# Taking two units' own terms from feature rows: a fused attention and two-layer product kernel on one core

## The chip, the core and the metric

The kernel runs on one core of a Trainium2 chip. The core has five engines with a queue each: PE (matrix products), DVE (vector), ACT (scalar functions and copies), POOL (a second vector engine) and SP, which here only issues transfers. Sixteen DMA engines carry the transfers. The metric is the device time of one execution in microseconds. Three runs of the kernel before gave 769.85, 770.53 and 771.16 us; the median is 770.53.

## What is computed

The reference has three parts. First a linear attention with a decaying state, for 4 batches of 8 heads, 768 steps, 48 features:

```python
state = zeros((B, H, D, D))
for t in range(S):
    kt, vt, rt, wt = k[:, :, t], v[:, :, t], r[:, :, t], w[:, :, t]
    cur = einsum('bhd,bhe->bhde', u[None] * kt, vt)
    y[:, :, t] = einsum('bhd,bhde->bhe', rt, state + cur)
    state = wt[..., None] * state + einsum('bhd,bhe->bhde', kt, vt)
```

Then, on the 3072 rows of the result with 384 columns, `((x @ w1) * (x @ w2) @ w3) @ w_out` with 1024 inner columns, and on what that gives, `max(x @ v1, x @ v2, x @ v3) @ v_out` with 768 inner columns. The weights come in 64 bits.

The step's *own term* is what `cur` adds to `y[t]`: the sum over the features of r·k·u at step t, times v at step t. The change is about how this one number for each step and head is found.

## The kernel before

**Units.** The attention is cut into eight units of 384 steps (half a batch each), and a unit into four pairs of heads (`j` = 0 to 3; k0 to k3 below means the four pairs of a unit, written `k = (u, j)` in the code). Within a pair, 384 steps are six chunks of 64. The two heads of a pair stand in partitions 0 to 47 and 64 to 111.

**Feature rows.** `dm` is one tile per pair with a row for each feature: the decays w, the keys k (in reversed order of time) and the queries r (forward). It is loaded by two DMAs of 48 rows (L303), each row 1159 numbers long. DVE scans the decays backwards (`sf`, L345) and forwards (`e`, L352); POOL multiplies keys (`kk`, L356) and queries (`x1`, `x2`, L370 and L372) by them.

**Token rows.** `tok` is a second copy of r and k, with a row for each step (128 partitions, 2304 bytes each), loaded at L312. POOL forms r·k (`rk`, L314) and r·k·u (`rku`, L316); a sum over each row gives six numbers per partition, `c`: on DVE in one instruction (L329), or, in unit 1 alone (`DIAG_ACT`), on ACT in six (L327). POOL then writes them on the diagonal of each chunk's 64 x 64 matrix, which stands in the free half of `x1` and `x2` (`dg0`, `dg1`, L380).

**Products of a pair.** PE forms the chunk matrices (`qk`, L392 and L393), DVE copies their lower triangles beside the diagonal (L405), PE transposes `kk` (`tr`, L398) and forms the states (`u`, L459), and at last the outputs (`y`, L417 and L418), which go in two parts to `xT` (L427, L428). The fourth pair's outputs go to `xT` by DMA (`xp`, L435).

**Weights.** At the start, `w3` and `w_out` are multiplied with each other once (`wmul`, L826): 64 products of 128x384 in full f32, two for each of the eight pieces of `w3`, called halves below (four products each). They need the three `wo` tiles (two for the first half, the third for the second) and a piece of `w3`. Each of these 1024-column tiles is made from 64-bit words by three DVE instructions (L784, L787, L790). `w1` and `w2` (`w12`) follow in eight tiles, each in two parts of 384 columns, with a copy on ACT (L817) and a subtraction on POOL (L818).

**The long products.** For each unit and each of eight column tiles PE forms two groups of nine products (`Aa`, `Ab`, from `xT` and `w12`) and one of nine (`B`, from `gs` and `W`); a first product of unit u needs all of `xT`. After the last unit the second layer's groups (C and D) follow. All of these come from one helper and stand at L509.

**What sets the order.** All instructions are recorded as events with an engine, an estimated cost, what they need, what buffers they claim and, for some, a due time. A planner (`Plan`, L48) walks through them in a time of its own and writes each engine's instructions in the order of their start there. On the chip each engine then works through its own list in that order, and waits at the head of the list. Its constants are numbers in the code: the rate it assumes for a transfer (`RATE`), and the due times (`T_A`, `UNIT`, `T_W`, `D_W`, `LEAD`, `T_V`). A change of any of them can move instructions on all engines. SP's transfers are in that same order.

Of the kernel before, what the change touches and what calls it, by code (L numbers as in the profile page):

```python
# [9 lines left out]
F32 = mybir.dt.float32  # L10
# [21 lines left out]
O_K, O_R = NW, NW + T  # L32
DMW = NW + 2 * T

# [13 lines left out]
class Plan:  # L48
# [5 lines left out]
    HOP = 0.12  # L54
    RATE = 285e3
    LAND = 3.0
# [154 lines left out]
class Net:  # L211
# [4 lines left out]
    def constants(self, pool):  # L216
# [46 lines left out]
    NX = 4  # L263
    DIAG_ACT = (1,)

# [8 lines left out]
    def plan_unit(self, u):  # L274
# [10 lines left out]
        for j in range(NJ):  # L285
# [3 lines left out]
            def dm(k=k):  # L289
                return self.dm[slot["dm", *k][0]]  # L290
# [14 lines left out]
            add(("dm", *k), "SP", 1.0, load, after=last, size=96 * DMW * 4,  # L305
                claims=[("dm", [(w, *k) for w in ("sf", "e", "x1", "x2", "kk", "wchk0", "wchk1")])])
            lt = [("tok", u, j - 1)] if j else [("tok", u - 1, NJ - 1)] if u else []
# [8 lines left out]
            add(("rku", *k), "POOL", 0.80, lambda k=k: G.tensor_mul(  # L316
                tok(k)[:, 0], tok(k)[:, 0], self.ub[:, k[1], :].unsqueeze(1).to_broadcast([128, NC, D])),
                [("rk", *k)], lock=True)

            def cd(k=k):  # L320
                return self.cd[slot["diag", *k][0]]

            def diag(k=k):
                if k[0] in self.DIAG_ACT:
                    for c in range(NC):
                        t = tok(k)[:, 0, c]
                        SC.activation(out=t, in_=t, func=AF.Copy, accum_out=cd(k)[:, c:c + 1])  # L327
                else:
                    V.tensor_reduce(out=cd(k), in_=tok(k)[:, 0], axis=AX.X, op=ALU.add)  # L329

            add(("diag", *k), *(("ACT", 1.6) if u in self.DIAG_ACT else ("DVE", 0.45)), diag,
                [("rku", *k)], claims=[("c", [("dg0", *k), ("dg1", *k)])])

# [32 lines left out]
            def r(k, p, q):  # L366
                return dm(k)[p:q, O_R:].rearrange("p (c t) -> p c t", t=C)

# [659 lines left out]
def layout(inputs):  # L1028
# [10 lines left out]
    for i, h in enumerate((1, 0)):  # L1039
# [4 lines left out]
        rd[:, :, i] = rows(R)  # L1044
    dm = np.concatenate([x.reshape(NU, NJ, 2 * D, -1) for x in (we, kd, rd)], axis=3)
    tok = np.stack([R[:, :, :, :, ::-1], K[:, :, :, :, ::-1]], axis=2)
# [17 lines left out]
    res["u2"] = u2  # L1064
    res |= {"dm": dm, "tok": tok, "v1": v1, "v2": v2, "u": ub, "w3": w3, "wo": wo, "w12": w12}
    for n in ("moe_w1", "moe_w2", "moe2_w1", "moe2_w2", "moe2_w3", "moe2_w_out"):
# [20 lines left out]
```

## Time and profile before

| | |
|---|---|
| median of three runs | 770.53 us |
| the profiled execution | 770.51 us |
| its span, first to last instruction | 768.7 us |
| mean granted share of PE's clock | 0.983 |
| PE busy | 737.4 us, 96% of the span |
| weight loads on PE | 696.9 us, 91% |
| DVE, ACT, POOL busy | 447.0, 332.9, 243.5 us |
| moved by DMA | 102.94 MB, mean 134 GB/s |

The span is cut in 40 slices in this part of the page; a digit is the busy share in tenths, and PEclk is the clock granted to PE in tenths of full speed:

```
PE   3499999999999999999999999999999999999996
DVE  7798999677876777585547887323232323232222
PEclk8689999999999999999999999999999999999999
DMA  7988753445354543344024447576767200000001
```

A slice is 19.2 us. PE is filled from the third slice to the last but one, and DVE is above 70% in the first six; the DMA engines are busiest in the first four. The two levels of PE's clock are 1.2 GHz (0.5 in the profile) and 2.4 GHz (1.0).

### The profile page before, as it was taken

Reading aid. Unit: us, or ns where it says so; the run is one execution under the profiler, and the core shown is the slowest. Engines: PE = TensorE matmul, PEld = TensorE weight load, DVE = VectorE, ACT = ScalarE, POOL = GpSimd, SP = SyncE. Lnnn points to the kernel's source line nnn. Section 1 sums busy time; section 2 is a strip of 40 time slices with the busy share of each in tenths; the row PEclk is TensorE's granted clock in tenths of the full one; section 3 lists DMA queues with packets and bytes.
Section 4 is the critical chain, followed back from the end, with each engine's and each line's share of the span. In section 5 each row is a group of like instructions: output and inputs, shape, how many; then the busy total and the mean of one; then the engine's idle time right before and its main releaser. Section 6 shows DMA issues by size and latency. Waiting matters only on the chain.

```text
span 768.7 us, 14960 instructions
## 1 busy us (share of the span) xinstructions
PE 737.4 (96%) x5994; PEld 696.9 (91%) x5994; DVE 447.0 (58%) x731; ACT 332.9 (43%) x798; POOL 243.5 (32%) x293
## 2 busy tenths in 40 slices
PE   3499999999999999999999999999999999999996
PEld 1366788999999999999999999999999999999996
DVE  7798999677876777585547887323232323232222
ACT  2244556354635445354343335667766422222211
POOL 4484678655575565545002332000000000000000
PEclk8689999999999999999999999999999999999999
DMA  7988753445354543344024447576767200000001
GB/s 252 308 274 251 218 185 85 109 110 151 98 139 126 126 93 111 92 125 93 2 82 172 129 159 280 197 256 204 245 204 242 76 32 1 32 1 32 1 31 35
DMA packets 30588, 102.94 MB, mean 134 GB/s; under 512 B 4272, under 2 KB 7472, under 8 KB 30512
## 3 DMA queue, kind: packets, MB, share of 16 engines
q1 hardware_dynamic: 30368, 101.72, 43.2%
q8 instruction: 49, 0.80, 0.4%
q14 instruction: 27, 0.22, 0.1%
q10 hardware_dynamic: 144, 0.20, 0.1%
HBM read 91.28 MB, written 8.26 MB: 129 GB/s over the span
## 4 chain that ended last, share of the span: by engine, by line
PE 93%; DVE 5%; issue 1%; POOL 1%; DMA 0%; ACT 0%; SPq 0%; DVEq 0%; POOLq 0%
PE bank L509 40%; PE rot L509 38%; PE bank L826 6%; PE bank L417 3%; PE bank L392 2%; PE bank L459 1%; PE bank L398 1%; PE bank L393 1%; DVE conv L784 1%; DVE x L405 1%; DMA dm<-in_dm 0%; DVE conv L787 0%; DVE e L352 0%; POOL w L818 0%; DVE gs L856 0%
## 5 line engine op out<-in xcount | busy, mean ns | idle before, releaser
L509 PE MATMUL rot<-xT,w 128*128 128x384 f32 x1152 | 217.2, 339 | 0.9 <-POOL w L818 0.7
L509 PEld LDWEIGHTS rot<-xT,w 128*128 128x128 f32 x1152 | 198.6, 188 | 4.3 <-POOL w L818 1.3
L509 PE MATMUL bank<-x2s,v 128*128 128x384 f32 x684 | 125.6, 336 | 0.0
L509 PEld LDWEIGHTS bank<-x2s,v 128*128 128x128 f32 x684 | 119.0, 188 | 0.0
L509 PE MATMUL bank<-gs,W 128*128 128x384 f32 x576 | 112.6, 338 | 1.2 <-DVE gs L856 1.2
L509 PEld LDWEIGHTS bank<-gs,W 128*128 128x128 f32 x576 | 100.7, 188 | 2.5 <-DVE gs L856 1.8
L956 DVE TENSOR_TENSOR m<-m,bank 128x384 f32<-128x384 f32 x58 | 32.1, 554 | 109.2 <-PE bank L509 99.9
L509 PE MATMUL bank<-vo,ms 128*128 128x384 f32 x432 | 83.5, 337 | 0.0
L509 PE MATMUL rot<-x2s,v 128*128 128x384 f32 x450 | 83.5, 336 | 0.0
L509 PEld LDWEIGHTS rot<-x2s,v 128*128 128x128 f32 x450 | 78.4, 188 | 0.0
L509 PEld LDWEIGHTS bank<-vo,ms 128*128 128x128 f32 x432 | 76.5, 187 | 0.2 <-DVE ms L963 0.2
L961 ACT CAST ms<-m 128x384 fp32r<-128x384 f32 x48 | 24.6, 513 | 96.7 <-DVE m L956 96.4
L850 ACT COPY a<-rot 128x384 f32<-128x384 f32 x64 | 30.6, 478 | 77.6 <-PE rot L509 77.4
L956 DVE TENSOR_TENSOR m<-m,rot 128x384 f32<-128x384 f32 x38 | 21.0, 554 | 66.9 <-PE rot L509 61.0
L854 ACT CAST gs<-g 128x384 fp32r<-128x384 f32 x64 | 32.9, 515 | 61.9 <-DVE g L852 60.3
L852 DVE TENSOR_TENSOR g<-a,rot 128x384 f32<-128x384 f32 x64 | 35.3, 551 | 41.4 <-PE rot L509 40.9
L356 POOL TENSOR_TENSOR kk<-dm,sf 112x384 f32<-112x384 f32 x32 | 32.0, 1006 | 62.3 <-PE bank L393 26.7
L405 DVE COPY_PREDICATED x<-later,bank 64x384 f32<-64x384 uint32 x64 | 37.9, 592 | 22.8 <-PE bank L393 21.8
L826 PE MATMUL bank<-wo,piece 128*128 128x384 f32 x128 | 46.9, 525 | 3.4 <-DVE piece L790 3.4
L856 DVE TENSOR_TENSOR gs<-g,gs 128x384 fp32r<-128x384 f32 x64 | 41.0, 642 | 15.0 <-ACT gs L854 14.8
L370 POOL TENSOR_TENSOR x<-dm,e 48x384 f32<-48x384 f32 x32 | 30.9, 966 | 44.5 <-DVE e L352 27.1
L826 PEld LDWEIGHTS bank<-wo,piece 128*128 128x128 f32 x128 | 25.7, 206 | 21.0 <-DVE piece L790 3.5
(117 smaller groups left out, 1080.1 us busy)
## 6 DMA issues: line engine op xcount, KB each, us to landing
dm<-in_dm SPq DMA_DIRECT2D x64, 217.3 KB, 4.1
tok<-in_tok SPq DMA_DIRECT2D x32, 288.0 KB, 4.0
wst<-in_w SPq DMA_DIRECT2D x8, 1024.0 KB, 8.7
top<-in_w SPq DMA_DIRECT2D x8, 1024.0 KB, 5.0
vst<-in_moe_w SPq DMA_DIRECT2D x9, 768.0 KB, 4.7
top<-in_moe_w SPq DMA_DIRECT2D x9, 768.0 KB, 4.4
wst<-in_w SPq DMA_DIRECT2D x8, 768.0 KB, 5.2
top<-in_w SPq DMA_DIRECT2D x8, 768.0 KB, 4.2
```

The costliest lines, as they stand in the source:

```text
L356: add(("kk", *k), "POOL", 0.86, lambda k=k: G.tensor_mul(kk(k).rearrange("p (c t) -> p c t", t=C), dm(k)[0:PR, O_K:O_R].rearrange("p (c t) ...
L370: add(("x1", *k), "POOL", 0.94, lambda k=k: G.tensor_mul(x1(k)[64:PR], r(k, 64, PR), e(k)[64:PR, :, 0:C]), [("e", *k)], after=lx, lock=Tru ...
L405: add((f"qk{i}", *k), "DVE", 0.59, lambda k=k, x=x, p=p: V.copy_predicated(x(k)[p:p + 64], self.later.bitcast(U32)[p:p + 64].unsqueeze(1). ...
L417: nc.tensor.matmul(ps[0:48, s], self.TA[:, o], x1(k)[:, c, :], start=True, stop=True)
L509: r = self.nc.tensor.matmul(ps, w[p], x[q], start=first and i == 0, stop=last and i == 2)
L826: nc.tensor.matmul(ps[:, 0:DM], t[:, jt * 128:(jt + 1) * 128], wo[:, jt * DM:jt * DM + DM], start=jt == 0, stop=jt == FT - 1)
L850: add(("a", g), "ACT", 0.48, lambda g=g: SC.copy(at[slot["a", g][0]], rot[slot["Aa", g][0]][:, 0:T]), [("Aa", g)], claims=[("a", [("m", g)])])
L852: add(("m", g), "DVE", 0.555, lambda g=g: V.tensor_mul(gt[slot["m", g][0]], at[slot["a", g][0]], rot[slot["Ab", g][0]][:, 0:T]), [("a", g) ...
L854: add(("h", g), "ACT", 0.51, lambda g=g: SC.copy(gst[slot["h", g][0]][:, 0], gt[slot["m", g][0]]), [("m", g)], claims=[("gs", [("B", g)])])
L856: add(("l", g), *self.on("l", u, 0.56, 0.95), lambda g=g, u=u: self.eng("l", u).tensor_sub(gst[slot["h", g][0]][:, 1], gt[slot["m", g][0]] ...
L956: V.tensor_max(t, t, p)
L961: add(("mh", h), "ACT", 0.51, lambda h=h: SC.copy(p2["ms"][slot["mh", h][0]][:, 0], p2["m1"][slot["mx", h, 0][0]]), [("mx", h, 2)], claims ...
```

## The change

For units 0 and 1 (`DIAG_PE`) the token copy is no longer loaded. POOL multiplies the keys of `dm` by its queries, read backwards, to a tile of 112 x 384 (`rk`, in the space of `tok`). PE multiplies each chunk of it with a column of u by features (`dp`: twelve products per pair, 48 rows, 64 columns of weights, one moving column), which lands in PSUM as six numbers per step row; ACT copies them to `c`. The other units keep their way, and all of them now sum on DVE. A small tile `uf` with u by features is loaded first. A row of `dm` is filled up with zeros from 1159 to 1184 numbers. The planner's rate and due times are changed too.

```diff
-DMW = NW + 2 * T
+DMW = (NW + 2 * T + 31) // 32 * 32
-    RATE = 285e3
+    RATE = 380e3
-    DIAG_ACT = (1,)
+    DIAG_PE = (0, 1)
...
-            add(("tok", *k), "SP", 0.55, lambda k=k: nc.sync.dma_start(tok(k), a["tok"][k]), after=lt,
-                size=128 * 2 * NC * D * 4, claims=[("tok", [("diag", *k)])])
-            add(("rk", *k), "POOL", 0.80, lambda k=k: G.tensor_mul(tok(k)[:, 0], tok(k)[:, 0], tok(k)[:, 1]),
-                [("tok", *k)], lock=True)
...
+            if u in self.DIAG_PE:
+                def rk(k=k):
+                    return self.tok[slot["rk", *k][0]].rearrange("p a c d -> p (a c d)")[0:PR, 0:T]
+
+                add(("rk", *k), "POOL", 0.95, lambda k=k: G.tensor_mul(
+                    rk(k), dm(k)[0:PR, O_K:O_R], dm(k)[0:PR, O_R + T - 1:O_R - 1:-1]), [("dm", *k)], after=lt, lock=True,
+                    claims=[("tok", [("dp", *k)])])
+
+                def dp(k=k):
+                    ps = self.ab[slot["dp", *k][0]]
                     for c in range(NC):
...
+                        q = slice(T - c * C - C, T - c * C)
+                        nc.tensor.matmul(ps[0:64, c:c + 1], rk(k)[64:PR, q], self.uf[64:PR, k[1]:k[1] + 1], start=True, stop=True)
+                        nc.tensor.matmul(ps[64:128, c:c + 1], rk(k)[0:48, q], self.uf[0:48, k[1]:k[1] + 1], start=True, stop=True)
+
+                add(("dp", *k), "PE", 0.35, dp, [("rk", *k)], claims=[("ab", [("diag", *k)])], kind="s")
+                add(("diag", *k), "ACT", 0.2, lambda k=k: SC.copy(cd(k), self.ab[slot["dp", *k][0]][:, 0:NC]), [("dp", *k)],
+                    claims=[("c", [("dg0", *k), ("dg1", *k)])])
+            else:
...
-    T_A, UNIT, T_W, D_W, LEAD, T_V = 29.5, 37.7, 18.9, 2.0, (1.0, 16.9, 3.6, 35.2), 20.0
+    T_A, UNIT, T_W, D_W, LEAD, T_V = 32.8, 38.3, 20.5, 3.1, (0, 16.9, 5.1, 35.2), 10.0
...
+        nc.sync.dma_start(self.uf, a["uf"])
         nc.sync.dma_start(self.ub, a["u"])
```

**SP, from the start.** `wst` is a tile of 64-bit weights (from `wo` or `w3`, shown as `in_w`), `dm` the feature rows of a pair, `V`, `TA` and `TB` the values, `tok` the token rows. Before:

```order
L743 DMA ub_96<-in_u 128x192
L303 DMA dm_128<-in_dm 48x1159 x2
L303 DMA dm_129<-in_dm 48x1159 x2
L758 DMA wst_121<-in_wo 128x2x512
L758 DMA wst_122<-in_wo 128x2x512
L758 DMA wst_123<-in_w 128x2x512
L441 DMA V_151<-in_v 128x1152
L312 DMA tok_130<-in_tok 128x576
L312 DMA tok_131<-in_tok 128x576
L445 DMA TA_152<-in_v 64x1152
L446 DMA TB_153<-in_v 64x1152
```

The same place with the change:

```order
L758 DMA uf<-in_uf 112x4
L759 DMA ub_97<-in_u 128x192
L774 DMA wst_122<-in_wo 128x2x512
L304 DMA dm_129<-in_dm 48x1184 x2
L304 DMA dm_130<-in_dm 48x1184 x2
L774 DMA wst_123<-in_wo 128x2x512
L774 DMA wst_124<-in_w 128x2x512
L456 DMA V_152<-in_v 128x1152
L460 DMA TA_153<-in_v 64x1152
L461 DMA TB_154<-in_v 64x1152
L774 DMA wst_122<-in_wo 128x2x512
L774 DMA wst_123<-in_w 128x2x512
```

The first weight tile now stands ahead of the feature rows, the two token loads are gone, and the third `wo` tile and the second piece of `w3` follow at once.

**SP, the rows that follow**, where the feature rows of k2 and k3 of unit 0 are loaded. Before:

```order
L303 DMA dm_128<-in_dm 48x1159 x2
L758 DMA wst_121<-in_wo 128x2x512
L303 DMA dm_129<-in_dm 48x1159 x2
L758 DMA wst_122<-in_w 128x2x512
L758 DMA wst_123<-in_w 128x2x512
```

With the change, behind the rows shown above:

```order
L774 DMA wst_124<-in_w 128x2x512
L304 DMA dm_129<-in_dm 48x1184 x2
L774 DMA wst_122<-in_w 128x2x512
L304 DMA dm_130<-in_dm 48x1184 x2
L774 DMA wst_123<-in_w 128x2x512
```

The rows of k2 (`dm_129`) stand behind two more weight tiles than before, and those of k3 (`dm_130`) behind three more.

**DVE, after the first memsets.** `conv`, `wo` and `piece` are the three steps of a weight tile, `sf`, `inv` and `e` the scans of a pair. Before:

```order
L345 SCALAR_TENSOR_TENSOR sf_134<-dm_128,first 112x390
L350 RECIPROCAL inv_76<-sf_134 112x6
L352 SCALAR_TENSOR_TENSOR e_132<-dm_128,inv_76 112x390
L345 SCALAR_TENSOR_TENSOR sf_135<-dm_129,first 112x390
L350 RECIPROCAL inv_77<-sf_135 112x6
L352 SCALAR_TENSOR_TENSOR e_133<-dm_129,inv_77 112x390
L784 TENSOR_SCALAR conv<-wst_121 128x1024
L787 SCALAR_TENSOR_TENSOR conv<-wst_121,conv 128x1024
L790 SCALAR_TENSOR_TENSOR wo<-wst_121,conv 128x1024
L784 TENSOR_SCALAR conv<-wst_122 128x1024
```

With the change:

```order
L800 TENSOR_SCALAR conv<-wst_122 128x1024
L803 SCALAR_TENSOR_TENSOR conv<-wst_122,conv 128x1024
L806 SCALAR_TENSOR_TENSOR wo<-wst_122,conv 128x1024
L360 SCALAR_TENSOR_TENSOR sf_135<-dm_129,first 112x390
L360 SCALAR_TENSOR_TENSOR sf_136<-dm_130,first 112x390
L800 TENSOR_SCALAR conv<-wst_123 128x1024
L803 SCALAR_TENSOR_TENSOR conv<-wst_123,conv 128x1024
L806 SCALAR_TENSOR_TENSOR wo<-wst_123,conv 128x1024
L365 RECIPROCAL inv_76<-sf_135 112x6
L800 TENSOR_SCALAR conv<-wst_124 128x1024
L803 SCALAR_TENSOR_TENSOR conv<-wst_124,conv 128x1024
L806 SCALAR_TENSOR_TENSOR piece_125<-wst_124,conv 128x1024
```

The first weight tile is made ahead of the first scan, and the two `e` scans now follow the first piece of `w3`.

## Rows read from the trace of the kernel before

**Rows 1.** The page's first part: busy time of each engine, its share, instructions.

```profile
PE 737.4 (96%) x5994; PEld 696.9 (91%) x5994; DVE 447.0 (58%) x731; ACT 332.9 (43%) x798; POOL 243.5 (32%) x293
```

**Rows 2.** Stretches of the span: busy time of each engine, granted clock, DMA.

```profile
core 0: us, PE busy (x) PEld busy (x) DVE busy (x) ACT busy (x) POOL busy (x), PEclk, DMA share, GB/s
0.00:10.00 10.00, 5.51 (x8) 2.31 (x8) 5.15 (x15) 1.56 (x2) 2.90 (x14) 1.00 0.54 116
10.00:20.00 10.00, 1.33 (x6) 0.80 (x7) 9.69 (x10) 3.37 (x12) 5.97 (x6) 0.59 1.01 398
22.00:24.00 2.00, 0.00 (x0) 0.00 (x0) 1.93 (x3) 0.26 (x1) 1.92 (x3) 0.50 1.05 229
24.00:26.00 2.00, 1.09 (x2) 0.79 (x3) 1.58 (x3) 0.00 (x0) 0.69 (x3) 0.50 1.00 180
30.00:40.00 10.00, 3.78 (x51) 2.86 (x48) 9.17 (x11) 2.40 (x7) 4.52 (x5) 0.78 1.03 326
100.00:140.00 40.00, 37.71 (x475) 34.49 (x475) 34.33 (x57) 20.21 (x50) 34.59 (x44) 1.00 0.45 127
350.00:500.00 150.00, 150.00 (x1107) 148.24 (x1106) 95.21 (x138) 65.85 (x132) 31.87 (x24) 1.00 0.42 140
```

**Rows 3.** The chain that ended last, to 90 us: start, duration, work.

```profile
24.91 4.76 PE bank L826 x8
...
38.74 7.09 PE bank L826 x16
...
49.45 0.20 PE bank L392
...
50.99 5.36 PE bank L826 x16
56.35 0.29 PE bank L398 x3
...
65.29 20.84 PE bank L826 x64
```

**Rows 4.** DVE in order of time: start, duration, work, idle time before and its releaser.

```profile
8.43 0.97 DVE L345 TENSOR_TENSOR_SCAN sf<-dm,first 112x390 f32<-112x390 f32 x1 [3.01 <-DMA dm<-in_dm]
...
13.58 1.20 DVE L784 TENSOR_SCALAR conv<-wst 128x1024 uint32<-128x1024 uint32 x1
...
17.33 1.23 DVE L784 TENSOR_SCALAR conv<-wst 128x1024 uint32<-128x1024 uint32 x1
...
41.36 1.22 DVE L790 SCALAR_TENSOR_TENSOR piece<-wst,conv 128x1024 uint32<-128x1024 uint32 x1
```

**Rows 5.** Groups of instructions by line: count, then busy us and mean ns.

```profile
L345 DVE TENSOR_TENSOR_SCAN sf<-dm,first 112x390 f32<-112x390 f32 x32 | 36.8, 1150 | 8.4 <-DMA dm<-in_dm 8.4
L352 DVE TENSOR_TENSOR_SCAN e<-dm,inv 112x390 f32<-112x390 f32 x32 | 36.8, 1149 | 0.7
...
L356 POOL TENSOR_TENSOR kk<-dm,sf 112x384 f32<-112x384 f32 x32 | 32.0, 1006 | 62.3 <-PE bank L393 26.7 <-DVE sf L345 24.2 <-PE rot L509 5.9
...
L329 DVE TENSOR_REDUCE c<-tok 128x6 f32<-128x288 f32 x28 | 12.3, 445 | 3.6 <-POOL x L380 2.5 <-POOL tok L316 1.0
```

**Rows 6.** SP's queue in order of time: start, duration, transfers issued.

```profile
4.11 2.12 SPq L303 DMA_DIRECT2D dm<-in_dm  x4
...
7.25 0.47 SPq L758 DMA_DIRECT2D wst<-in_w  x1
...
15.25 0.98 SPq L303 DMA_DIRECT2D dm<-in_dm  x2
```

**Rows 7.** Transfers issued from 6 to 9 us: count, KB each, us to landing.

```profile
wst<-in_w SPq DMA_DIRECT2D x1, 1024.0 KB, 11.2
```

**Rows 8.** Transfers issued from 13 to 16 us, likewise.

```profile
dm<-in_dm SPq DMA_DIRECT2D x2, 217.3 KB, 10.7
```

**Rows 9.** The chain: the first work behind unit 1's last outputs.

```profile
123.99 1.77 PE rot L509 x9
```

**Rows 10.** SP's queue: the transfers of unit 1's last outputs.

```profile
125.60 3.71 SPq L435 DMA_DIRECT2D xT<-y  x6
```

More of the change, by code (lines that the diff above doesn't have):

```diff
@@ L242, in constants @@
         self.ub = pool.tile([128, NJ, D], F32, name="ub")
+        self.uf = pool.tile([PR, NJ], F32, name="uf")
     def att_tiles(self):
@@ L305, in plan_unit, with first @@
             add(("dm", *k), "SP", 1.0, load, after=last, size=96 * DMW * 4,
-                claims=[("dm", [(w, *k) for w in ("sf", "e", "x1", "x2", "kk", "wchk0", "wchk1")])])
-            lt = [("tok", u, j - 1)] if j else [("tok", u - 1, NJ - 1)] if u else []
+                claims=[("dm", [(w, *k) for w in ("sf", "e", "x1", "x2", "kk", "wchk0", "wchk1") + ("rk",) * (u in self.DIAG_PE)])])
+            def first(u):
+                return "rk" if u in self.DIAG_PE else "tok"
+            lt = [(first(u), u, j - 1)] if j else [(first(u - 1), u - 1, NJ - 1)] if u else []
@@ L320, in cd @@
             def cd(k=k):
                 return self.cd[slot["diag", *k][0]]
-            def diag(k=k):
-                if k[0] in self.DIAG_ACT:
-                    for c in range(NC):
[L326 to L332, printed above, removed]
+            if u in self.DIAG_PE:
[6 more added lines that the diff above has]
+                    ps = self.ab[slot["dp", *k][0]]
+                    for c in range(NC):
+                        q = slice(T - c * C - C, T - c * C)
[5 more added lines that the diff above has]
+            else:
+                add(("tok", *k), "SP", 0.55, lambda k=k: nc.sync.dma_start(tok(k), a["tok"][k]), after=lt,
+                    size=128 * 2 * NC * D * 4, claims=[("tok", [("diag", *k)])])
+                add(("rk", *k), "POOL", 0.80, lambda k=k: G.tensor_mul(tok(k)[:, 0], tok(k)[:, 0], tok(k)[:, 1]),
+                    [("tok", *k)], lock=True)
+                add(("rku", *k), "POOL", 0.80, lambda k=k: G.tensor_mul(
+                    tok(k)[:, 0], tok(k)[:, 0], self.ub[:, k[1], :].unsqueeze(1).to_broadcast([128, NC, D])),
+                    [("rk", *k)], lock=True)
+                add(("diag", *k), "DVE", 0.45, lambda k=k: V.tensor_reduce(out=cd(k), in_=tok(k)[:, 0], axis=AX.X, op=ALU.add),
+                    [("rku", *k)], claims=[("c", [("dg0", *k), ("dg1", *k)])])
@@ L366, in r @@
             def r(k, p, q):
-                return dm(k)[p:q, O_R:].rearrange("p (c t) -> p c t", t=C)
+                return dm(k)[p:q, O_R:O_R + T].rearrange("p (c t) -> p c t", t=C)
             lx = [("x1", u, j - 1)] if j else [("x1", u - 1, NJ - 1)] if u else []
@@ L1044, in layout @@
         rd[:, :, i] = rows(R)
-    dm = np.concatenate([x.reshape(NU, NJ, 2 * D, -1) for x in (we, kd, rd)], axis=3)
+    dm = np.zeros((NU, NJ, 2 * D, DMW), np.float32)
+    dm[..., :NW + 2 * T] = np.concatenate([x.reshape(NU, NJ, 2 * D, -1) for x in (we, kd, rd)], axis=3)
+    uf = np.zeros((PR, NJ), np.float32)
+    for h, p in ((1, 0), (0, 64)):
+        uf[p:p + D] = u.reshape(NJ, 2, D)[:, h].T
     tok = np.stack([R[:, :, :, :, ::-1], K[:, :, :, :, ::-1]], axis=2)
@@ L1064, in layout @@
     res["u2"] = u2
-    res |= {"dm": dm, "tok": tok, "v1": v1, "v2": v2, "u": ub, "w3": w3, "wo": wo, "w12": w12}
+    res |= {"dm": dm, "tok": tok, "v1": v1, "v2": v2, "u": ub, "w3": w3, "wo": wo, "w12": w12, "uf": uf}
     for n in ("moe_w1", "moe_w2", "moe2_w1", "moe2_w2", "moe2_w3", "moe2_w_out"):
```

3 lines of the change are left out of this document (removed).

## The prediction

> **What bounds the kernel now.** I read four views in this order: the busy times, stretches of the span, the chain of waits, and the queues of DVE and SP. PE is busy for 96% of the span [rows 1]. The stretches show where the missing 4% lie: PE works 1.33 of the ten us from 10 us and 3.78 of the ten from 30 us, but 150.00 of 150.00 from 350 us on [rows 2]. In the chain PE's work follows on itself from 38.74 us [rows 3]. So from there the time is the sum of PE's work, and the start-up before it is the only large idle time. What PE waits for then is DVE: 9.69 busy of ten us in the same stretch where PE has 1.33 [rows 2]. A tile of 64-bit weights costs DVE 17.33 - 13.58 = 3.75 us [rows 4]. The first product of weights starts at 24.91 [rows 3], and the second piece of `w3` ends at 41.36 + 1.22 = 42.6 [rows 4]. DVE itself first waits 3.01 us for the feature rows [rows 4], which SP issued at 4.11 [rows 6].
>
> From 100 to 140 us PE lacks 40 - 37.71 = 2.3 us, with DVE at 34.33 of 40 [rows 2]: DVE is the next limit there.
>
> **Padding.** Loads of feature rows fill 48 partitions each. Where they run, the DMA engines are full at 180 GB/s; where the value loads of 64 partitions run (rows of 4608 bytes), 229; at 10 to 20 us, mostly loads to 128 partitions, 398 [rows 2]. So a load to half of the partitions goes at about half rate, whatever the length of its rows. Padding alters rows from 4636 to 4736 bytes and no partition. I take 200 GB/s for the padded loads, near both rows; the bounds are 180 and 398.
>
> The Trainium skill (SBUF — State Buffer, Door 1: The DMA port swizzle) says that the bandwidth depends on how many ports the partitions reach, and that one half of the partitions reaches every second port. By that rule the padded loads stay at half rate, and the trace (180 and 229 against 398) agrees.
>
> **The start, walked through with the new order.** A load is 1.05 MB per weight tile, 0.91 MB for the two pairs' rows, 0.59 MB for V and for TA with TB. A landing comes about 1 us behind its last byte: 4.14 MB stand in the queue up to the tile issued at 7.25 [rows 6]; 1.16 MB had moved by 10 us, the rest at 398 GB/s takes 7.5 us [rows 2], so 17.5, and it landed at 7.25 + 11.2 = 18.45 [rows 7].
>
> Transfers: an issue takes 0.47 [rows 6], so the first `wo` tile, behind two small loads, moves from about 2.2 to 4.8 and lands at 5.8. Feature rows of k0 and k1 move to 9.35 (last landing 10.4), the second `wo` tile to 12.0 (landed 13.0), the first `w3` tile to 14.6, V to 16.1, TA and TB at 229 to 18.7, the third `wo` tile to 21.3 (landed 22.3). The two token loads, 0.59 MB, are gone.
>
> DVE: first tile 5.8 to 9.55, two scans at 1.15 [rows 5] to 11.85, wait, second tile 13.0 to 16.75, a reciprocal of 0.2, first `w3` piece to 20.7. So the first product of weights comes at 20.7 instead of 24.91. Then a reciprocal and a scan to 22.05, the third `wo` tile 22.3 to 26.05, a scan to 27.2, the second piece of `w3` to 31.0 instead of 42.6.
>
> PE: the first half of the first piece costs 4.76 [rows 3], at the granted 0.5 that a mostly idle PE has there [rows 2]; the second half follows at 26.1; both `qk` of k0 and k1 stand before 31.0. From 31.0 PE has work.
>
> **Sum.** (a) Before, PE is filled from 38.74, and pays 7.09 for two halves that take 5.36 at 50.99 [rows 3], since the clock had fallen in the pause (mean 0.78 from 30 to 40 [rows 2]). 38.74 + 1.73 - 31.0 = 9.5 us earlier. With less than 2 us of pause I count no such fall.
> (b) At that point PE has one half of 20.84 / 8 = 2.6 us more behind it, and two transposes of 0.29 less [rows 3]: 2.0 more.
> (c) PE's list holds the transposes, `dp` and `u` of k2 and k3 ahead of the third piece. The `kk` of k3 needs a scan that DVE reaches at 36.9, then 1.15 and 1.01 on POOL [rows 5]: 39.1, while PE is through at about 38.1. Idle 1.0; bounds 0 and 3.
> (d) Twelve products for each of eight pairs are added. The first two sets lie in the start's idle time; six stand where PE is full. Two `qk`, of as many products and as wide weights, take 50.99 - 49.45 = 1.54 [rows 3], with one change of kind in it of 5.36 - 2 x 2.6 = 0.15, so 0.70 each. They stream 64 columns where `dp` has one, so `dp` may cost less; the three transposes at 0.29 are my lower bound, twice 0.70 the upper one, and I take 0.70, since weights are loaded alike: 4.2. Ten more changes of kind in PE's list, at 0.15: 1.5. Together 5.7.
> The Trainium skill (TensorE: Matmul & The Clock Gate, LDWEIGHTS) puts a load of weights at its columns divided by 1.2 in ns, so 53 ns for 64 columns: it does not depend on the moving side. By this `dp` would cost 0.64 (an estimate) and the sum change by 0.4 us; the row is near it.
> (e) Hidden or elsewhere: POOL's `rk` reads the queries backwards. No row has that on POOL; on DVE the backward scan takes 1150 ns and the forward one 1149 [rows 5], so I take 1.01 as for `kk` (bounds 1.0 and 2.0; each of the first four beside DVE's tiles, which go on meanwhile). It replaces two multiplications of the token rows. DVE loses four reductions of 0.445 [rows 5], ACT its unit-1 sums: no path ends there. The 100 to 140 us stall of 2.3 may shrink, since DVE is ahead too: its list up to the last part of `w12` is 3.8 us shorter (six reductions, two subtractions), and early waits go. I count 0 of it; bounds 0 and 2.3. The second layer's weights keep their place beside the last groups: nothing.
>
> Gain 9.5 + 2.0 - 1.0 - 5.7 = 4.8 us. The profiled execution took 770.51 (768.7 of span, 1.8 around it), as good as the median 770.53: 765.7.
>
> **Rivals.**
> *Padding does double the rate.* Then 0.91 MB move in 2.3 instead of 4.6 us; DVE's wait of 1.15 before the second tile and the 0.25 before the third go, and (c) shrinks by some 0.2: 1.6 more, 764.1. For it: 180 is below the value loads' 229, so some of the loss may be the rows' odd start. Against it: 229 is no 398. Chance 0.12.
> *The gain is given back at unit 1's hand-over.* In PE's new order five groups of long products stand between unit 1's last outputs and the first product that needs all of its `xT`, where seven stood. Before, outputs ended at 123.99 [rows 9], the six transfers were issued from 125.60 for 3.71 us [rows 10], and with a landing of 2 to 3 us the way takes 7.5 to 8.5 us. Five groups of nine (1.77 [rows 9] at most) and a few small products cover 9. If DVE, full there, comes 4 us late with the last subtraction, PE stands for 3 to 4: 769.5 to 770.5, no change. For it: DVE's 34.33 of 40. Against: DVE should be further ahead than PE. Chance 0.13.
> *Slower: k3's feature rows come late.* SP now issues them behind three weight tiles more, of which one waits for DVE. I have them issued at 29.2 and landed at 34.7; DVE wants them at 36.9, and the third piece stands behind them in DVE's and PE's lists. Loads of this kind took 10.7 us from issue to landing when the queue was full [rows 8]: landed at 39.9, DVE 3 us late, PE idle for 4 and its clock down again (1.7 as in (a)): 770.4. From there on each us more is a us lost: at 13 us, 772.7, slower. It decides at about 11 us. For it: DMA is full there in both. Against: in the new queue only some 2 MB stand ahead at that time. Chance 0.13, of which 0.10 slower.
>
> **How the numbers follow.** The forecast keeps 0.62: 763 to 768.5, by the bounds of (c), (d) and (e). With 0.2% (1.5 us, what a measurement can tell) as the border, faster is nearly all of the forecast (0.59), the first rival (0.12) and a piece of the second (0.03): 0.74. No change: the rest of the forecast (0.03), of the second (0.10) and the third (0.03): 0.16. Slower 0.10. The range reaches from 762.0, where a cheap `dp` and the vanished stall meet, to 771.0, into the third rival.
>
> **What would show it.** First product of weights near 20.7, second piece near 31; PE in the chain without break from about 31; the granted clock at 1.0 from about 26 on, instead of falling again at 36 to 42; a set of `dp` at 0.6 to 0.8 where PE is full; feature rows still at about 200 GB/s. I am wrong if pieces come as late as before, if PE pauses over 3 us after 31, or if the same lead at 85 us is gone by 140.

## The result: one per cent slower, and the profile after

The changed kernel took 779.05 us (median of four executions, 776.78 to 779.92), the kernel before 770.85 beside it: a ratio of 1.010, 95% interval 1.0073 to 1.0128. The forecast was 765.7. The profiled execution of the changed kernel took 776.78 us, with a span of 775.1; it was the fastest of the four.

The page's first part, to be held against [rows 1]:

```profile
PE 750.6 (97%) x6186; PEld 707.2 (91%) x6186; DVE 440.1 (57%) x727; ACT 329.7 (43%) x758; POOL 244.9 (32%) x285
```

PE has 192 records more, the 96 `dp` products (an f32 product leaves two records), and is busy for 13.2 us more. The `dp` records fill 8.0 of them; most of the rest is the same work done more slowly, `wmul` alone 48.8 us for 46.9. Where, the stretches show (columns as in [rows 2]):

```profile
20.00:30.00 10.00, 8.82 (x87) 5.69 (x88) 8.88 (x10) 0.70 (x2) 3.53 (x5) 1.00 1.03 358
30.00:40.00 10.00, 7.83 (x46) 4.36 (x44) 9.65 (x13) 3.41 (x11) 5.83 (x7) 1.00 0.86 258
40.00:50.00 10.00, 8.51 (x106) 6.04 (x107) 7.34 (x8) 4.57 (x15) 8.38 (x13) 0.66 0.63 197
50.00:60.00 10.00, 10.00 (x71) 5.93 (x71) 7.88 (x9) 2.84 (x8) 7.53 (x11) 1.00 0.61 181
70.00:80.00 10.00, 9.36 (x114) 6.25 (x115) 9.72 (x17) 2.49 (x7) 3.58 (x3) 0.83 0.84 238
120.00:130.00 10.00, 8.55 (x93) 7.83 (x90) 9.75 (x13) 4.97 (x12) 9.29 (x14) 1.00 0.03 8
```

The start did become busier: 7.83 of the ten us from 30 us where [rows 2] has 3.78. But the granted clock falls twice, to a mean of 0.66 from 40 to 50 us and 0.83 from 70 to 80. The 1.00 from 20 to 30 us is no reading: this trace's first record of the clock is at 25.94 us, and what stands ahead of it is shown as 1.00. PE in order of time has the first half of the first piece still mostly at the lower level and the second at the higher, 4.43 and 2.85 us for eight records each:

```profile
22.71 4.43 PE L842 MATMUL bank<-wo,piece 128*128 128x384 f32 x8 [1.09 <-DVE piece L806]
...
27.92 2.85 PE L842 MATMUL bank<-wo,piece 128*128 128x384 f32 x8
```

The chain of waits of the changed kernel, cut to these two places, with what leads to the first of them (start, duration, work):

```profile
11.98 12.51 DMA wst<-in_wo
...
28.25 0.97 DVE e L367
...
30.28 0.91 POOL x L387
...
31.21 0.31 SPq L304
31.57 6.88 DMA dm<-in_dm
...
38.59 1.58 POOL tok L324
40.26 0.90 POOL x L385
...
41.23 0.90 POOL x L387
42.13 0.88 POOL kk L371
43.06 0.84 PE bank L413 x3
43.92 0.45 ACT kt L424
44.41 1.53 PE bank L474 x40
45.94 4.73 PE bank L842 x8
...
70.00 0.48 PE bank L413 x3
70.48 0.14 PE bank L332
...
72.86 0.21 PE bank L332
...
73.73 12.21 PE bank L842 x32
```

The third `wo` tile is issued at 11.98, when DVE has freed its buffer, and lands at 24.49 (forecast 22.3). `e` of k1 stands behind it in DVE's list, `x2` of k1 (L387) needs `e`, and only then is the buffer of k3's rows free: they are issued at 31.21 and land at 38.45. (In the order shown ahead of the prediction, k2's rows too stand behind three more weight tiles than before, six for three, and not behind two.) POOL then has `rk` of k3 and `x1`, `x2` of k2 at the head of its list, so `kk` of k3 comes at 43.0. Behind that stand `tr` (L413, 0.84 where [rows 3] has 0.29), `u` (L474), and the half at 45.94, which takes 4.73 us for 2.6. From 69 us on it happens again, with unit 1's `tr`, `dp` (L332) and `u`: the four halves from 73.73 take 12.21 us.

DVE of the changed kernel at the start, columns as in [rows 4]:

```profile
8.21 1.23 DVE L800 TENSOR_SCALAR conv<-wst 128x1024 uint32<-128x1024 uint32 x1 [2.74 <-DMA wst<-in_wo]
...
21.43 1.22 DVE L806 SCALAR_TENSOR_TENSOR piece<-wst,conv 128x1024 uint32<-128x1024 uint32 x1
...
31.63 1.22 DVE L806 SCALAR_TENSOR_TENSOR piece<-wst,conv 128x1024 uint32<-128x1024 uint32 x1
...
41.01 1.22 DVE L806 SCALAR_TENSOR_TENSOR piece<-wst,conv 128x1024 uint32<-128x1024 uint32 x1
```

The second piece is there at 32.85 instead of 42.6 [rows 4], the third at 42.2. The lead is easiest to see by counting, in the trace, the records of products of weights (128 in all) that have begun by a time:

| by (us) | 40 | 45 | 50 | 60 | 70 | 80 | 90 |
|---|---|---|---|---|---|---|---|
| before | 11 | 22 | 32 | 56 | 79 | 110 | 128 |
| after | 32 | 32 | 39 | 64 | 80 | 95 | 113 |

Twenty-one records are 21/8 of a half of 2.6 us, so 6.8 us of lead at 40 us. At 70 us it is all but gone, at 80 the changed kernel is behind. To take other products in, I weight all records of PE, `dp` left out, by what they take in the full stretches of before: the changed kernel is 6.5 us ahead at 40, 1.7 at 50, 0.4 at 70, then 3.8 behind at 80, 3.7 at 140 and 6.0 at 350. The largest single loss, 4.2 us, falls between 70 and 80 us, where two sets of `dp` (1.5 us) stand beside the pauses and the clock. The last 2.3 are a third loss, told below.

### The profile page after: what moved, and what is told of

It is laid out like the page before. It is cut to its first block, busy times and chain, and to the rows that moved or that the text cites. A ratio compares the mean times of both kernels' runs of the same rounds, so it can differ in the third digit from the quotient of the medians.

```text
span 775.1 us, 15286 instructions
## 1 busy us (share of the span) xinstructions
PE 750.6 (97%) x6186; PEld 707.2 (91%) x6186; DVE 440.1 (57%) x727; ACT 329.7 (43%) x758; POOL 244.9 (32%) x285
## 4 chain that ended last, share of the span: by engine, by line
PE 91%; DMA 5%; DVE 2%; POOL 1%; SPq 0%; ACT 0%; issue 0%; POOLq 0%; DVEq 0%; ACTq 0%
PE bank L524 40%; PE rot L524 37%; PE bank L842 5%; PE bank L432 3%; DMA wst<-in_wo 2%; PE bank L407 2%; PE bank L474 2%; DMA dm<-in_dm 2%; PE bank L413 1%; DMA tok<-in_tok 1%; PE bank L408 1%; PE bank L332 0%; PE bank L433 0%; DVE conv L803 0%; DVE conv L800 0%
## 5 line engine op out<-in xcount | busy, mean ns | idle before, releaser
L842 PE MATMUL bank<-wo,piece 128*128 128x384 f32 x128 | 48.8, 538 | 1.8 <-DVE piece L806 1.8
L390 ACT ACTIVATE wjunk<-dm,bias 112x391 bf16<-112x391 f32 x64 | 40.0, 625 | 20.8 <-DMA dm<-in_dm 20.0
```

The source lines that it names most:

```text
L390: add((f"wchk{i}", *k), "ACT", 0.81, lambda k=k, i=i, sc=sc: SC.activation(out=self.wjunk[:, 0:NW], in_=we(k), func=AF.Relu, bias=self.bia ...
L842: nc.tensor.matmul(ps[:, 0:DM], t[:, jt * 128:(jt + 1) * 128], wo[:, jt * DM:jt * DM + DM], start=jt == 0, stop=jt == FT - 1)
```

## Experiments

Times are medians of 4 to 12 executions, the kernel before beside them; the ratio is to that. The changed kernel's own ratio comes from four executions and is known to 0.28%, 2.1 us, so a run within some 2.5 us of its 779.05 can hardly be told from it by the time alone.

| run | us | before | ratio, 95% |
|---|---|---|---|
| new way, old numbers | 774.86 | 770.93 | 1.0055 (1.0037 to 1.0073) |
| old way, new numbers | 779.00 | 770.93 | 1.0105 (1.0087 to 1.0122) |
| new way, old rate | 776.38 | 770.86 | 1.0070 (1.0056 to 1.0084) |
| padding alone | 771.55 | 770.86 | 1.0009 (1.0000 to 1.0018) |
| two sets, old numbers | 771.19 | 770.86 | 1.0003 (0.9994 to 1.0011) |
| four sets, old numbers | 772.01 | 770.86 | 1.0016 (1.0007 to 1.0026) |
| `dp` cut short | 776.36 | 770.93 | 1.0060 (1.0041 to 1.0079) |
| rows of k3 earlier | 778.33 | 770.93 | 1.0093 (1.0077 to 1.0110) |
| before, less DVE | 770.53 | 771.20 | 0.9995 (0.9986 to 1.0004) |
| after, less DVE | 779.20 | 771.20 | 1.0106 (1.0091 to 1.0121) |
| pauses filled | 773.86 | 771.20 | 1.0038 (1.0022 to 1.0055) |
| second pause filled | 776.97 | 771.13 | 1.0080 (1.0064 to 1.0095) |
| third piece first | 779.92 | 771.13 | 1.0118 (1.0103 to 1.0133) |
| the same, second pause filled | 780.09 | 771.13 | 1.0114 (1.0097 to 1.0130) |
| before, pause filled | 770.38 | 771.13 | 0.9991 (0.9982 to 0.9999) |
| two sets, pause filled | 771.41 | 771.20 | 0.9999 (0.9990 to 1.0008) |
| filled, `dp` cut short | 773.55 | 770.37 | 1.0034 (1.0021 to 1.0047) |
| the same, not padded | 772.62 | 770.37 | 1.0028 (1.0015 to 1.0041) |

### The new way apart from the new numbers

New way with old numbers:

```diff
-    RATE = 380e3
+    RATE = 285e3
-    T_A, UNIT, T_W, D_W, LEAD, T_V = 32.8, 38.3, 20.5, 3.1, (0, 16.9, 5.1, 35.2), 10.0
+    T_A, UNIT, T_W, D_W, LEAD, T_V = 29.5, 37.7, 18.9, 2.0, (1.0, 16.9, 3.6, 35.2), 20.0
```

> The changed kernel with the planner's rate and due times of before (285e3; 29.5, 37.7, 18.9, 2.0, ...): the new way of the own terms alone, in an order planned with the old numbers. Theory A (the new order costs the time: k3's rows come late, PE pauses and its clock falls, and the same again at unit 1's small products): without the new numbers the time is before's 770.9, plus six sets of dp at 0.75 us = 4.5, less 0 to 4 us of a lighter DVE: 767 to 775. Theory B (the dp products and what they do to PE cost the time, in any order): 777 to 781. Theory C (the padded rows and POOL's longer multiply cost it): 777 to 781 too.

The same two lines the other way round in the kernel before:

> The kernel before with the new rate and due times alone; token rows, row sums and unpadded rows as they were. Theory A: the new numbers plan too fast a DMA for this start in either kernel, so the order suffers here too: 774 to 780. Theories B and C: no dp and no padding, so no loss: 766 to 772.

And the rate alone put back in the changed kernel:

> The changed kernel with the planner's rate of before alone (285e3 instead of 380e3), the new due times kept. Theory R (the rate is what harms: the plan believes in loads that land sooner than they do, and puts what waits for them at the heads of the queues): most of the 4 us between this kernel with all new numbers (779.0) and with all old ones (774.9) goes: 773 to 776. Theory D (the due times harm: they set the order of tiles, pieces and small products): 777 to 781.

The new way costs 3.9 us in the old order, so no theory was right alone: A's range held for it (at its upper edge), and part of the loss is the numbers'. These cost 4.2 us on top of the new way (779.05 - 774.86). The rate alone put back gives 2.7 of them, at the border of what can be told; 776.38 lies between the ranges of theories R and D, and both missed. On the kernel before the numbers cost 8.1, and in part at the same place: weighted as above, that kernel is 6.5 us ahead at 40 and 0.6 at 60, with a pause and a fall of the clock between, and it has no `dp` and no padding. So the new order alone gives the early start back. A stretch of it, and PE in order of time with the idle time before:

```profile
40.00:50.00 10.00, 5.86 (x34) 3.47 (x35) 6.38 (x10) 2.93 (x10) 9.01 (x12) 0.66 0.76 233
```

```profile
44.14 4.59 PE L826 MATMUL bank<-wo,piece 128*128 128x384 f32 x8 [4.98 <-DVE W L831]
```

Its second loss is at another place than the changed kernel's, at unit 1's outputs:

```profile
118.72 0.31 PE L417 MATMUL bank<-x,TA 112*48 112x64 f32 x2 [3.61 <-ACT TA L493]
```

POOL's chain of states ends there at 118, and PE waits for it. So two orders by the same numbers share the first loss and not the second; the costs do not add up across kernels.

### How many sets, and the padding

The rows are filled up, with the planner told the old size, so that the order of before stays:

```diff
-DMW = NW + 2 * T
+DMW = (NW + 2 * T + 31) // 32 * 32
...
-            add(("dm", *k), "SP", 1.0, load, after=last, size=96 * DMW * 4,
+            add(("dm", *k), "SP", 1.0, load, after=last, size=96 * (NW + 2 * T) * 4,
...
```

> The kernel before with rows of dm filled up from 1159 to 1184 numbers, the planner told the old size, so that every engine's order is word for word that of before. Theory P (part of the 4 us that the new way costs in the old order is the padding): 772 to 775. Theory S (that cost is the dp sets on PE, 8 x 0.5 to 0.75): 770 to 772; if the padded loads move at twice the rate, 769 to 770.

Then the new way for some pairs alone, the rest with token rows, in orders by the old numbers:

```diff
...
-    DIAG_PE = (0, 1)
+    DIAG_PE = ((0, 0), (0, 1))
+    DIAG_ACT = (1,)
...
```

> The changed kernel with the old rate and due times, and the new way for the first two pairs of unit 0 alone (two sets of dp instead of eight); the other six pairs of units 0 and 1 keep token rows, unit 1 sums on ACT as before. Theory S (a set costs 0.5 to 0.75 us where PE is full and nothing in the idle start): both sets lie in the idle start, 769.5 to 772. Theory P or another fixed cost of the new way: 773 to 775.

```diff
...
-    DIAG_PE = (0, 1)
+    DIAG_PE = ((0, 0), (0, 1), (0, 2), (0, 3))
+    DIAG_ACT = (1,)
...
```

> As the run with two sets, but the new way for all four pairs of unit 0. Theory S: two sets in the idle start, two where PE is nearly filled: 0.5 to 1.5 us above the run with two sets, 770.5 to 773, and two to three below the one with eight (774.9). A fixed cost of the new way: 773 to 775, as with two.

The padding is worth nothing or costs up to 0.18%. Two sets cost nothing, four 1.15 us, eight 3.9. From four to eight, all of them in unit 1, where PE is nearly full, it is 774.86 - 772.01 = 2.85 us, 0.71 a set (each in an order of its own, so this is a step of a ladder and not a price by itself). Theory S held in all three.

The products taken away in the changed kernel's own order:

```diff
-                    for c in range(NC):
+                    for c in range(NC if k[0] == 0 and k[1] < 2 else 1):
```

> The changed kernel in its own order, but six of the eight sets of dp (k2 and k3 of unit 0, all of unit 1) issue 2 of their 12 products; the own terms of the other chunks are left out, so the output is not the reference's. Theory A: 6 x (0.75 - 0.15) = 3.6 us go, the pauses stay: 774 to 776.5. Theory B: the whole loss goes, and the lead from the start shows: 766 to 771. Theory C: 774 to 776.5 as in A.

2.7 us less, 0.45 a set, against 0.6 expected; theory B fell, and A and C, which had the same range, are not told apart by this.

### Earlier rows for k3, less work for DVE

The list of moves, without the loop that makes them:

```diff
+        (('e', 0, 1), 'behind', ('e', 0, 0)),
+        (('f', ('w3', 3)), 'behind', ('dm', 0, 3)),
+        (('sf', 0, 3), 'behind', ('e', 0, 2)),
+        (('qk1', 0, 0), 'behind', ('sf', 0, 3)),
+        (('kk', 0, 3), 'behind', ('rk', 0, 3)),
+        (('wchk1', 0, 3), 'behind', ('kt', 0, 2)),
+        (('wchk0', 0, 3), 'behind', ('kt', 0, 2)),
```

> The changed kernel with seven events moved in its order, nothing else: DVE makes e of k1 right behind e of k0 (ahead of the third wo tile), SP issues k3's rows ahead of the weight tile that stood before them, DVE scans k3 ahead of the third piece's second step, POOL makes kk of k3 ahead of x1 and x2 of k2, ACT makes the two checks of k3's rows behind kt of k2. Theory A: rows of k3 issued at 28.6 instead of 31.2, kk of k3 done at 39 instead of 43.0, third piece's first half at 42.5 instead of 45.9 and at full clock (2.6 instead of 4.7 us): 3 to 6 us less than the changed kernel, 773 to 776. Theory B or C: no change, 778 to 780.

No gain that can be told from nothing (778.33), so theory A's 773 to 776 missed. `kk` of k3 did come earlier (40.4 in place of 43.0), but PE now waits 2.7 us for a copy of k0's triangle that DVE makes behind k3's scan, and its clock falls all the same:

```profile
40.00:50.00 10.00, 8.83 (x107) 6.83 (x108) 8.56 (x10) 5.03 (x16) 6.00 (x10) 0.54 0.66 196
```

So I asked whether DVE sets the pace. In both kernels, the first two steps of the seven later pieces of `w3` treat 128 of 1024 columns, which leaves out a part of the weights' low bits:

```diff
+        def short(w, name):
+            return 128 if name[0] == "w3" and name[1] else w
...
```

> The kernel before with less work for DVE: of the seven later pieces of w3 the first two steps treat 128 of 1024 columns; that part of the weights' low bits is left out. Some 7 x 2.1 = 15 us leave DVE's list, the order stays. A control for the next run. Second piece 2 us earlier, and PE's idle 2.3 us from 100 to 140 us gone: 766 to 769.

> The changed kernel with the same work left out (part of the weights' low bits). Theory V (DVE's list is what gave the early start back: PE ran ahead only because DVE had put off k2's and k3's scans and the first masks, and PE then waits for it): with 15 us less on DVE most of the lead stays, and what is left against the light kernel before is the dp sets less the start: 0 to +4 us against that run, 767 to 772. Theory O (waits that are not DVE's, k3's rows, ACT's copies, small products one behind the other, cost it): 6 to 8 us above the light kernel before, 772 to 777.

Neither moved, and every range given for them missed: the kernel before took 770.53, the changed one 779.20, 8.7 above, where theory O had 6 to 8. DVE has 11.8 us less to do in the kernel before and 13.5 in the changed one, and that is worth nothing in either; theory V, which was the prediction's view of the start, fell for DVE's work from the second piece on. What DVE does ahead of that (three `wo` tiles, the first piece) was not made lighter, so the two runs say nothing of it. Nor did PE's idle time from 100 to 140 us in the kernel before shrink (37.73 busy for 37.71). DVE of the changed kernel with less work shows why the third piece is no earlier: it waits for k3's rows as well, with the third piece's last step behind them in its list, and ends that piece at 42.1 as before.

```profile
35.49 0.60 DVE L420 COPY_PREDICATED x<-later,bank 64x384 f32<-64x384 uint32 x1
38.43 0.97 DVE L360 TENSOR_TENSOR_SCAN sf<-dm,first 112x390 f32<-112x390 f32 x1 [2.35 <-DMA dm<-in_dm]
...
40.89 1.22 DVE L809 SCALAR_TENSOR_TENSOR piece<-wst,conv 128x1024 uint32<-128x1024 uint32 x1
```

### Useless work in the pauses

Products of no use are put in PE's list where it waits: seven (14 records in the trace), though the expectation says eight. They release nothing and lengthen the list, so I take it that they can make the kernel faster by PE's clock alone.

```diff
+    FILL = {('dp', 0, 2): (390, 390), ('dp', 0, 3): (200,), ('u', 0, 1): (390,), ('tr', 1, 1): (390,), ('u', 1, 0): (128,), ('dp', 1, 1): (256,)}
...
+            for w in self.FILL.get(n, ()):
+                nc.tensor.matmul(bank[4][0:PR, 0:w], self.ident[0:PR, 0:PR], ...)
```

> The changed kernel with eight products of no use put in PE's list where PE waits: three ahead of dp of k2 and k3, one ahead of u of k2 and k3, three among tr, u and dp of unit 1's first two pairs (390, 390, 200, 390, 390, 128, 256 columns, to an unused bank). Theory C (the clock that falls in the pauses costs much of the loss: the half at 45.94 takes 4.7 instead of 2.6 us, the four halves from 73.73 12.2 instead of 10.4): granted clock near 1.0 from 40 to 50 and 70 to 80 us, 774 to 776.5. Theory V: PE then waits longer for the next piece instead: 777.5 to 780.

773.86 us: 5.2 less than the changed kernel, the largest gain of a single edit. Stretches of this run:

```profile
40.00:50.00 10.00, 9.20 (x132) 6.18 (x133) 7.41 (x8) 4.37 (x15) 7.67 (x11) 0.83 0.65 208
...
70.00:80.00 10.00, 10.00 (x103) 6.54 (x100) 9.62 (x18) 2.05 (x6) 4.71 (x5) 1.00 0.74 221
```

Its chain, at the products that stood at 45.94 and 73.73:

```profile
46.69 2.78 PE bank L844 x8
...
72.73 10.52 PE bank L844 x32
```

The half takes 2.78 us for 4.73, the four halves 10.52 for 12.21, and the first long products of unit 0 start at 84.09 instead of 86.78. In the profiled executions this is 2.7 us at that point and 2.9 at the end. The medians differ by 5.2; why the other executions of the changed kernel are slower than the profiled one, its fastest, no trace shows. (The mean granted clock of an execution is no guide: the 0.992 of the profiled one counts as full what stands ahead of its first record.) Theory C held, 0.1 us under its range, but not in all it said of the clock: from 40 to 50 us the mean is 0.83. There the clock still falls, at the small products from 43.12 us, and is back ahead of the half at 46.69. The second pause alone:

> The changed kernel with these three useless products alone. Theory C, by the rows: four halves from 73.73 take 12.2 us at a granted 0.83 and would take 10.4: 776.5 to 778. If the first pause (40 to 50 us, granted 0.66) carries all of the 5.2 us: 778.5 to 779.5.

776.97, in theory C's range: 2.1 us less, which leaves 3.1 of the 5.2 for the first pause. By the time alone 2.1 can hardly be told from nothing; in the trace the four halves take 10.52 us again, and the half behind the first pause still 4.70.

The kernel before has a pause of 5.4 us of its own ahead of `tr` of k3 (PE of that kernel in order of time):

```profile
37.92 0.82 PE L398 MATMUL bank<-ident,kk 112*128 112x112 f32 x3 [5.42 <-POOL kk L356]
```

```diff
+    FILL = {('tr', 0, 3): (390, 390, 390, 390)}
```

> The kernel before with four useless products of 390 columns ahead of tr of k3 of unit 0, where PE waits 5.4 us; the two halves behind that wait take 7.09 us for 5.36. Theory C holds for the kernel before too: clock up at 38.7, 1.5 to 2 us less, 768.5 to 769.5, faster than both kernels. Theory L: 770.5 to 771.5.

It gained 0.7 us, at the border of what can be told, and not the 1.5 to 2 of theory C. Its clock is up, and PE then waits for the next piece (a stretch, and PE in order of time):

```profile
40.00:50.00 10.00, 8.39 (x76) 4.63 (x76) 9.81 (x12) 2.70 (x8) 8.21 (x12) 1.00 1.00 310
```

```profile
43.40 2.85 PE L828 MATMUL bank<-wo,piece 128*128 128x384 f32 x8 [1.61 <-DVE piece L792]
```

Four such products in the kernel with two sets, ahead of the second piece's first half and with rows of 1159 numbers again, were to beat both kernels and gained nothing:

> The kernel with two sets of dp, its rows of 1159 numbers again (same order), and four useless products of 390 columns ahead of the second piece's first half, where PE waits 3.46 us and then works 4.1 us for 2.6. If the clock of that half is lost time and the padding costs its 0.7: 768.5 to 770, faster than both kernels. If DVE's next piece ends the wait anyway: 770 to 771.5.

### Long products in place of the pause

Again the list of moves alone:

```diff
+        (('c3', ('w3', 2)), 'behind', ('c2', ('w3', 2))),
+        (('wl', 0), 'behind', ('c3', ('w3', 2))),
+        (('wmul', 2, 0), 'behind', ('wl', 0)),
+        (('wmul', 2, 1), 'behind', ('wmul', 2, 0)),
```

> The changed kernel with four events moved: DVE ends the third piece of w3 and the first subtraction ahead of k3's scan, and PE multiplies the third piece ahead of tr, dp and u of k2 and k3, which it waited for with nothing to do. Theory C (the pause and the clock that falls in it are the loss): PE busy and at full clock from 39.7 to 45, the small products find their operands there: u done at 49 instead of 45.9, but two halves done by then: 3 to 5 us less, 774 to 776. Theory L (the lead is given back wherever the small products stand): 777.5 to 780.

> As the run with the third piece first, and three products of no use (390, 128 and 256 columns) among tr, u and dp of unit 1's first two pairs, where the changed kernel pauses from 69 to 73.7 us. Theory C: both falls of the clock are gone: 772 to 775, 2 us below the run without them. Theory L: 777 to 780.

Both missed theory C's ranges, by 4 and 5 us (779.92 and 780.09), and are as theory L had it. The third piece is done by 45.8 at full clock, as I wanted (46 records of weights by 45 us in place of 32). Then the small products of k2 and k3 stand in a row with nothing between them, and the pause and the fall of the clock have moved by ten us (the run with the third piece first):

```profile
40.00:50.00 10.00, 8.36 (x90) 5.65 (x92) 8.18 (x10) 1.79 (x8) 4.27 (x6) 1.00 0.52 154
50.00:60.00 10.00, 7.71 (x79) 4.95 (x70) 7.12 (x9) 3.97 (x11) 7.74 (x13) 0.52 0.57 196
```

The three products in the second pause bring the four halves from 12.28 to 10.59 us here too, and yet give no time that can be told: what a filled pause is worth hangs on the order around it.

### Both causes taken away

> The changed kernel with the eight useless products of the run with filled pauses, and with 2 of 12 products in six sets of dp (the own terms of the other chunks are left out, so the output is not the reference's). If the two costs stand side by side: 779.05 - 5.2 - 2.7 = 771.2, between 770 and 772.5, the level of the kernel before. If the sets of dp cost mostly by the pauses around them, so that both runs took away the same thing: 773 to 774.

> The same with rows of 1159 numbers in the same order: what the padding cost in the old order, 0.7 us, less again: 769.5 to 771.5 if all three stand side by side. This leaves of the change the new order, without its pauses: at 770.9 or above it, the early start is worth nothing; below 769.5, it is worth what is below.

They do not stand side by side: with the pauses filled, the shorter sets gave nothing more that can be told (773.55, executions from 770.37 to 775.99). Fewer products leave longer pauses (PE busy for 5.09 of the 8 us from 38 to 46, for 6.84 with whole sets), so part of what a set costs and part of what a pause costs are the same time. Unpadded it is 772.62, still 0.28% above before; by the mark set beforehand the early start is worth nothing. In the profiled execution of the first of the two (773.52) the granted clock stays full from 25 to 760 us, in the first pause too, so what is left there is not the clock:

```profile
40.00:50.00 10.00, 7.69 (x99) 4.68 (x98) 8.45 (x11) 5.41 (x16) 9.06 (x13) 1.00 0.59 180
```

What is left points to the new numbers' later order, but no run takes that alone: weighted as above, the changed kernel loses 2.3 us between 140 and 350 us and these two 2.9 and 1.8; with old numbers the new way loses 0.3 with eight sets and 1.0 with four. A part is idle time of PE, as between 220 and 260 us, where the changed kernel has

```profile
220.00:260.00 40.00, 39.24 (x390) 37.63 (x388) 27.26 (x47) 19.08 (x50) 25.23 (x28) 1.00 0.54 135
```

(before: 39.97 of 40). The rest of it stays open.

## Why the prediction was wrong

**The sum's first term, (a), failed, and (c) with it.** The start went as forecast, 2 us late: first product of weights at 22.7 (forecast 20.7), second piece at 32.85 (31.0). The first tile landed later than I had it, and DVE began at 8.21, not 5.8. But 9.5 us of lead were booked as gained because PE had been unbroken behind 38.74 in the kernel before [rows 3], and I assumed it would be so behind 31 too, with 1.0 us of pause and no fall of the clock. In fact PE was idle for 2.7 of the 8 us from 38 to 46, and its clock was down from 43 to 50:

```profile
38.00:46.00 8.00, 5.33 (x105) 4.15 (x103) 7.70 (x10) 3.19 (x11) 6.84 (x7) 0.81 0.38 107
```

Idle time of 2.7 us lies inside (c)'s bounds of 0 and 3. The clock behind it, put at nothing, lies in no bound: the half took 4.73 us for 2.6, and behind the second pause, which the sum does not have, the four halves 12.21 for 10.4. The kernel before ran its `tr` of k2 and k3 in its idle start, with a wait of 5.42 us for POOL's `kk`, and its `u` of k2 and k3 found their operands ready; the lead moved these hops between engines to where PE should have been full. A second piece that is earlier is no lead of the whole program: of 6.5 us at 40 us, 0.4 were left at 70. The runs with k3's rows earlier and with the third piece first show that the waits can be pushed along, but did not go.

**The bound was misread.** I took DVE for what PE waits for at the start. With 12 to 13 us less of its work from the second piece on nothing changed, so there it was a link in a ring: DVE's third piece behind k3's scan, k3's rows behind POOL's `x2` of k1, and PE behind them all. Two landings are the longest links of the chain before 43 us, the third `wo` tile's (12.51) and k3's rows' (6.88). Whether DVE's work ahead of the second piece bounds the start, no run shows.

**The third rival named the place, not the price.** Landing took 7.2 us from the issue, far from the 11 at which it was to decide. But the rows were issued 2 us later than in my walk, and `rk`, `x1` and `x2` stood before `kk`: 4.5 us from landing to `kk`'s end, where I had 1.15 of a scan and 1.01 on POOL. Of a head of a queue I had costed the duration (e) and not what stands behind it; `rk`'s own 0.86 to 1.59 us were under the upper bound, four of the eight under the lower one of 1.0 too.

**"With less than 2 us of pause I count no such fall" was wrong.** PE's longest single pause from 38 to 46 us is 1.74, and the clock fell; added up they are 2.7, but in the kernel with four sets (last section) it fell behind two waits of 1.3 us together. What filled pauses gave back, 5.2 us, is most of the 8.2. The signs of being wrong did not catch this: the pieces came early, no pause was over 3 us, and the lead was gone before 85 us.

**What held.** (d), as a duration: a set of `dp` takes 0.67 to 0.87 us in the chain (70.48 to 71.15; 72.86 to 73.73) for 0.70 and a change of kind of 0.15, and the ladder's last step, 0.71 a set, is near. As a cost it was too high in the changed kernel, where cutting six sets short gave 0.45 each; two of the six stood in the first pause. Padding does not double the rate: while only feature rows move, the changed kernel has

```profile
8.00:9.00 1.00, 0.28 (x1) 0.00 (x0) 0.79 (x1) 0.00 (x0) 0.00 (x0) 1.00 1.02 199
9.00:10.00 1.00, 0.00 (x0) 0.00 (x0) 0.97 (x2) 0.00 (x0) 0.00 (x0) 1.00 1.00 179
```

with the DMA engines full. That holds for rows of 4608 to 4736 bytes; other lengths to half of the partitions no run here has.

Unit 1's hand-over costs nothing, so the second rival fell: the six transfers are issued from 134.45, and PE is full from 130 to 140 us and for 39.97 of the forty behind that. PE's one wait from 100 to 140 us is another, 1.45 us for DVE's `gs`; the kernel before has 1.18 for the same among its 2.3, so DVE was rightly seen as the limit there, and some 0.8 us of the idle time that (e) left open went. A stretch, PE and SP in order of time:

```profile
130.00:140.00 10.00, 10.00 (x98) 9.61 (x99) 8.60 (x18) 4.48 (x10) 7.77 (x10) 1.00 0.41 90
```

```profile
125.22 3.23 PE L524 MATMUL bank<-gs,W 128*128 128x384 f32 x17 [1.45 <-DVE gs L872]
```

```profile
134.45 3.71 SPq L450 DMA_DIRECT2D xT<-y  x6
```

(By its own rows the second rival's way is 7.3 to 8.3 us and not 7.5 to 8.5; nothing hangs on it.)

## What to carry to other kernels

When a start is made earlier, follow the small products with their hops between engines as well as the large ones: if they stood in the idle start, they will now stand in the full stretch, and PE pauses there. A pause can cost twice, by itself and by the clock behind it; putting useless products into it is a cheap experiment that tells the two apart, and shows as well where the clock is worth nothing since the next operand is late (0.7 us in the kernel before, nothing in the one with two sets). And numbers that set an order cannot be priced one by one: the same two lines cost 4.2 us in one kernel and 8.1 in the other.

## What was not expected of the hardware

The clock falls after pauses that are short one by one. In the kernel with four sets, stretches of 1 us at `tr` of unit 1's last two pairs:

```profile
102.00:103.00 1.00, 0.94 (x34) 0.81 (x28) 0.88 (x3) 0.51 (x1) 0.60 (x1) 1.00 0.73 166
103.00:104.00 1.00, 0.37 (x3) 0.29 (x3) 0.97 (x2) 0.00 (x0) 1.00 (x2) 1.00 0.93 332
104.00:105.00 1.00, 0.38 (x5) 0.30 (x3) 0.96 (x3) 0.44 (x1) 0.94 (x3) 1.00 0.94 386
105.00:106.00 1.00, 1.00 (x25) 0.87 (x24) 1.00 (x2) 0.44 (x1) 0.92 (x2) 0.76 1.11 411
106.00:107.00 1.00, 1.00 (x10) 0.88 (x7) 0.97 (x2) 0.00 (x0) 1.00 (x2) 0.50 1.08 213
```

No wait there is longer than 0.68 us, and PE is busy for 0.37 and 0.38 of two us; then the clock is at its lower level, 1.2 GHz, from 105.5 to 108.9 us, with PE at work all the while. Not every such group of waits does this: in the run with filled pauses and short sets, waits of 1.07, 1.05 and 1.26 us between 37 and 44 us left the clock at its upper level.

The Trainium skill (TensorE: Matmul & The Clock Gate, HAM oscillation — how this bites in real kernels) says that waits between short runs of products send the clock down again, so that the next run starts cold, and that an order which keeps PE busy cures it. The Trainium skill's case has waits of 3 to 5 us each; here none was over 1.74 in the first pause and none over 0.68 in the rows above, so for the length the measurement decides. That the work behind starts cold, the trace confirms (4.73 and 12.21 us against 2.78 and 10.52 with filled pauses). As for the cure, useless products helped here and two other orders did not.
